# A fused attention and expert kernel whose opening issues its loads, copies and subtractions in a new order

## The chip, the cores and the metric

The kernel runs on one core of a Trainium2 chip. The metric is the device time of one execution in microseconds (us); the time before is the median of three runs. The engines are named as the profile names them: PE multiplies matrices (PEld is its weight load), DVE, ACT and POOL do elementwise work, and SP only issues transfers. POOL issues transfers too, in the order of its other instructions.

## The reference

The inputs are q, k and v of shape 8 x 8 x 576 x 64 (batch, heads, positions, width), s of 8 x 8 x 576, and the weights of eight experts. For each of the 64 pairs of batch and head it computes causal attention with a bias:

```python
s_pos = np.maximum(s, 0.0)
cum = np.cumsum(s_pos, axis=-1)
bias = -(cum[:, :, :, None] - cum[:, :, None, :])
scores = np.where(causal, -1000000000.0, scores + np.minimum(bias, 0.0))
scores = scores - np.max(scores, axis=-1, keepdims=True)
attn = np.exp(scores)
attn = attn / (np.sum(attn, axis=-1, keepdims=True) + 1e-09)
return np.matmul(attn, v).astype(np.float32)
```

The 4608 rows of the result then go to one of eight experts each (a router by cosine similarity, two matrix products, a weight per row).

## The kernel before

**Work.** The 64 pairs are called heads here, numbered 0 to 63. Four heads are a group, eight a batch. `qkb0` to `qkb2` hold q and k of a group, transposed, in rows 0 to 63; rows 64 to 127 hold the running sums of s, ones and zeros, and the row maxima that a first pass finds. q and k are used in two parts, a rounded one and the rest: `QC` and `KC` hold for each head the other combinations of the two parts. For group 0 the rest is a subtraction on chip (`klow` on POOL, `qlow` on DVE, two heads at a time: pair 0 and pair 1). For later groups ACT writes the negated rounded values (`neg`), and an adding transfer (`addl`, issued by POOL) adds the original from memory; `hcopy` writes the other half.

**A head.** `s1` to `s4` multiply q and k for the maxima, and DVE reduces them (`sr`, `max4`). After two heads `mrow1`/`mrow2` turn the maxima and `sends` has SP write them into `qkb`. `ta_`, `tb_` and `tbl` compute the shifted scores, ACT takes the exponents (`expa`, `expb1`, into P), POOL writes their low part (`pl_`, into PL, a piece of 576 columns and one of 1024), and `pv` multiplies with v, which `emm` and `vcp` have prepared. The first pass runs three to five heads ahead.

**Order.** All of it stands in a manual schedule: each engine runs its instructions in the order in which the Python code emits them. `begin()` is the opening: the setup, the first pass of heads 0 to 2 (`rows`), then a loop over heads 0 to 2 (their scores, and the first pass of heads 3 to 5) and the first pass of head 6 with `pv(0)`. From head 3 on, `step(n)` does head n's scores, the first pass of a later head, and `pv(n - 2)`. Step n of PE begins with the mask product of `ta`.

**Queues around the change.** Group 1 (heads 4 to 7) goes to `qkb1` in two transfers, k at line 949 and q after `sends()` of the first maxima. `load(2)` is group 2's, `loadc` writes the sums, `krow` a row of ones, `qones` and `kzeros` fill the rows below, `setup2` writes borders, `setup3` and `setup4` the router's constants. `vsq` sums the squares of v on ACT, `vscale` makes a scale of them, which `vcp` needs.

Of the kernel before, what the change touches and what calls it, by code (L numbers as in the profile page):

```python
# [106 lines left out]
def main(ctx, tc, qkh, qkc, vtin, s_in, emb, tau, w1h, w2h, out, shared, nb):  # L107
# [49 lines left out]
    nc.vector.memset(zero, 0.0)  # L157
    nc.vector.memset(one, 1.0)

    def kzeros(i):  # L160
        nc.vector.memset(qkbs[i][64:128, QW:].bitcast(F32), 0.0)

    def round0(i):
        nc.scalar.copy(qkbs[0][0:64, 2 * SP * i:2 * SP * i + 2 * SP], qrs[i])
# [12 lines left out]
    nc.vector.memset(tiny, 1.0e-30)  # L177
    nc.vector.memset(tri0, 0.0)
    nc.vector.memset(tri, 1.0)
    kzeros(1)  # L180
    nc.vector.tensor_scalar(st, st, 0.0, 8.0, op0=ALU.max, op1=ALU.mult)
    nc.vector.tensor_tensor_scan(cum, st, st, 0.0, op0=ALU.add, op1=ALU.bypass)
    nc.vector.tensor_copy(chl[:, 0, :], cum)
    nc.vector.tensor_sub(chl[:, 1, :], cum, chl[:, 0, :].bitcast(F32))
    for i in range(2):
        nc.sync.dma_start(qkbs[0][64 + i:65 + i, QW:].bitcast(F32), chl[0:HG, i, :].bitcast(F32))
    nc.vector.memset(ones, 1.0)

    def masks():
# [54 lines left out]
    def load(g, o=slice(0, QW + KW)):  # L244
        if g >= NGg:
            return
        qkb = qkbs[g % 3]
        if g > 0:
            nc.gpsimd.dma_start(qkb[0:64, o], qkh[g][:, o], **(dict(max_dma_last_dim=4864) if g < 3 else {}))
        G[g] = dict(QB=qkb[:, 0:QW].rearrange("p (h s) -> p h s", h=HG), KB=qkb[:, QW:].rearrange("p (h s) -> p h s", h=HG))  # L250

    def loadc(g):
        if g == 1:
            for i in range(2):
                nc.gpsimd.dma_start(qkbs[1][64 + i:65 + i, QW:].bitcast(F32), chl[HG:2 * HG, i, :].bitcast(F32))
        elif 1 < g < NGg:
            nc.sync.dma_start(qkbs[g % 3][64:66, QW:].bitcast(F32), cumd[:, HG * g:HG * (g + 1), :].rearrange("x r s -> x (r s)").bitcast(F32))
# [73 lines left out]
    def klow(i):  # L331
        h = pair(i)
        psub(KCs[0][0:64, h], krs[i].rearrange("p (h s) -> p h s", h=2), G[0]["KB"][0:64, h].bitcast(F32))

    def qlow(i):
        h = pair(i)
        nc.vector.tensor_sub(QCs[0][64:128, h], qrs[i].rearrange("p (h s) -> p h s", h=2)[:, :, 64:SP], G[0]["QB"][0:64, h, 64:SP].bitcast(F32))

    def prep(n, k):
        g, c = n // HG, n % HG  # L340
# [90 lines left out]
    def mrow1(n):  # L431
        if 0 <= n < NH and n % 2:
            rq.append(partial(mrow2, n // 2))
# [509 lines left out]
    def begin():  # L943
        make_identity(nc, ident)
        masks()
        load(0)
        loadc(1)
        nc.gpsimd.dma_start(krs[1], qkh[0][:, QW + 2 * S:])
        load(1, slice(QW, QW + KW))
        krow(0)  # L950
        krow(1)
        ra, rb, rc, rd, re = rsetup()
        rb()
        hset(0)
        for i in range(2):
            round0(i)
            hcopy(0, False, i)
            hcopy(0, True, i)
            if i == 0:
                ra()  # L960
        qlow(0)
        klow(0)
        rows(0)
        rc()
        rd()
        qones(1)
        rows(1)
        rc()
        sends()
        load(1, slice(0, QW))  # L970
        re()
        klow(1)
        for p in range(2):
            loadt(0, pair(p))
        nc.sync.dma_start(cumd.rearrange("x r s -> r x s").bitcast(F32), chl.bitcast(F32))
        rows(2)
        hset(1)
        setup2()
        neg(1, True, 0)
        neg(1, True, 1)  # L980
        for n in range(3):
            m = n + 3
            ta_(n, m)
            sr(m, 3)
            expa(n)
            if n == 0:
                vsq(0, (0, 1))
            if n == 1:
                sends()
                neg(1, False, 1)  # L990
            if n == 2:
                vscale(0)
                fslot()
                while tasks:
                    slot()
                vcp(0, False)
                vcp(1, False)
            s2(m)
            tb_(n)
            sr(m, 2)  # L1000
            sr(m, 1)
            if n == 2:
                vcp(0, True)
                vcp(1, True)
            s3(m)
            if n == 1:
                r7s[0]()
            tbl(n)
            s4(m)
            expb1(n)  # L1010
            if n == 0:
                neg(1, False, 0)
            if n == 1:
                vsq(0, (2, 3))
            if n == 2:
                hcopy(1, True, 0)
            mrow1(m)
            if n == 1:
                qlow(1)
            if n < 2:  # L1020
                pl_(n, 0, 576, "p")
                if n == 0:
                    addl(1, True, pair(0))
                pl_(n, 576, 1600, "p")
            if n == 2:
                qones(2)
            if n == 0:
                addl(1, True, pair(1))
                load(2)
            if n == 1:  # L1030
                addl(1, False)
                emm(0)
                emm(1, om)
        m = 6
        kzeros(2)
        krow(2)
        s1(m)
        sr(m, 3)
        sends()
        s2(m)  # L1040
        pv(0, [0, 1, 2])
        sr(m, 2)
        sr(m, 1)
        s3(m)
        emm(2)
        pv(0, [3, 4])
        s4(m)
        hcopy(1, True, 1)
        vcp(2, False)
        hcopy(1, False, 0)  # L1050
        vcp(2, True)
        hcopy(1, False, 1)
        loadc(2)
        loadt(1, pair(0))
        pl_(2, 0, 576, "p")

    def step(n):
        m = n + LA - (n < 6)
        live = n < NH
        b0, b1, c8 = n // H, n // H + 1, n % H  # L1060
        prev = n - 1 < NH
        g, c = n // HG, n % HG
        if live and c == 0:
            hset(g + 1)
            load(g + 2)
            loadc(g + 2)
        if n == 4:
            setup4()
            setup3()
        fslot()  # L1070
        norm1(n - 3)
        if live:
            ta_(n, m)
        if prev:
            pl_(n - 1, 576, PS(n), "p")
        sr(m, 3)
        norm2(n - 3)
        sa(m)
        if live:
            expa(n)  # L1080
            prep(n, True)
        norm3(n - 3)
        if live:
            tb_(n)
        sr(m, 2)
        s3(m)
        if live:
            tbl(n)
        mslot()
        if prev and PS(n) < 1600:  # L1090
            pl_(n - 1, PS(n), 1600, "v")
        if n < NH - 1:
            wlow()
        k = n - NH + 8
        if k > 7:
            wsq((12, 14, 14)[k - 8])
        if live:
            emm(n)
        sb(n, m)
        sbr(m)  # L1100
        if n < NH:
            tail(n)
        if n == 5:
            s1(10)
            sr(10, 3)
            s2(10)
        pv(n - 2, [0, 1, 2])
        if rq:
            rq.popleft()()
        if n == 5:  # L1110
            sr(10, 2)
            sr(10, 1)
            s3(10)
        pv(n - 2, [3, 4])
        if n == 5:
            s4(10)
        if n >= NH:
            for f in (norm1, norm2, norm3):
                f(n - 2)
            if n == NH:  # L1120
                wlow(4)
            for _ in range(9 if n == NH + 2 else 2):
                slot()
            tail(n)
        if live:
            expb1(n)
            vcp(n, False)
        aslot()
        if live:
            prep(n, False)  # L1130
            vcp(n, True)
        if n == NH - 1:
            xcv(0, 0)
            for f in (norm1, norm2, norm3):
                f(n - 2)
            for t in range(1, 3):
                xtr(0, t, pxs())
                xcv(0, t)
        if k > 0:
            wsq((0, 2, 3, 6, 8, 8, 9, 10, 12, 14, 16)[k])  # L1140
            wcv((0, 0, 0, 0, 0, 1, 2, 2, 1, 2, 0)[k], True)
        brk[0] = False
        if n < NH:
            slots(4)
        if n in (3, 4, 5):
            vsq(1, ((0,), (1,), (2, 3))[n - 3])
        if H <= n < NH and 2 <= c8 < 6 and b1 < nb:
            vsq(b1, (c8 - 2,))
        if live and c8 == 6 and b1 < nb:
            vscale(b1)  # L1150
        if n == 3:
            loadt(1, pair(1))
        if H <= n < NH and c8 < 4:
            loadt(b1, c8)
        if n == NH - 8:
            wissue(3)
        for _ in range(SCN[c8] if n < NH - 22 else n - NH + 3 if NH - 3 < n < NH else 1 + (c8 > 5) + 4 * (n > NH - 6)):
            scatter()
        later()
        if live and c == 0:  # L1160
            addl(g + 1, True)
        if live and c == 1:
            addl(g + 1, False)
        mrow1(m)
        if live:
            pl_(n, 0, 576, "p")
# [288 lines left out]
```

## Time and profile before

| | us |
|---|---|
| median of three runs | 789.05 |
| lowest and highest | 788.06, 793.63 |
| the profiled execution | 785.73 |
| its span, first to last instruction | 784.0 |

Engines busy in the span: PE 762.7 us (97%), DVE 526.6, ACT 568.0, POOL 384.3. The page's slices show PE below 90% only in the first 60 us and in the last slices. [...] In a timeline each row gives start, duration, the instruction, and in brackets how long the engine idled before it and what ended that.

### The profile page before, as it was taken

To read this page: it belongs to the slowest core of one execution; us is meant where nothing else is said; L and a number is where in the kernel's file an instruction comes from. 1 tells how busy PE (TensorE), PEld (TensorE's weight loads), DVE (VectorE), ACT (ScalarE), POOL (GpSimd) and SP (SyncE) were. 2 spreads that over 40 slices of the span, in tenths; PEclk is the share of its full clock that TensorE was granted. 3 is DMA by queue.
4 is the path that set the end of the run, shared out by engine and by line. 5 is a ranking of instruction groups with operands and counts; after the bars stand their busy time and mean duration, and the time that the engine had idled before them with its cause. 6 is when DMAs were issued, how large, how long until landed. Compare 5 with 4: busy or idle time off the path is not lost. (4 is left out here: it accounts for less than half of the span.)

```text
span 784.0 us, 19399 instructions
## 1 busy us (share of the span) xinstructions
PE 762.7 (97%) x7276; PEld 572.0 (73%) x7276; DVE 526.6 (67%) x1774; ACT 568.0 (72%) x1011; POOL 384.3 (49%) x372
## 2 busy tenths in 40 slices
PE   8679999999999999999999999999999999999997
PEld 4679999999999999996576557466465574664753
DVE  8568888888888878868675657655665466556621
ACT  9568999999999999987665866837648468376410
POOL 9847788898989798885422121220221212302001
PEclk9789999999999999999999999999999999999999
DMA  5965879798889898764724665653855557645001
GB/s 120 205 152 98 177 167 209 174 211 174 206 174 216 174 210 181 195 211 154 233 85 129 177 187 161 153 192 105 196 187 102 173 161 148 199 98 142 12 15 55
DMA packets 76096, 123.79 MB, mean 158 GB/s; under 512 B 38806, under 2 KB 39210, under 8 KB 75140
## 3 DMA queue, kind: packets, MB, share of 16 engines
q0 software_dynamic: 19728, 69.68, 37.9%
q1 hardware_dynamic: 56272, 52.84, 25.0%
q8 instruction: 58, 0.95, 0.5%
q14 instruction: 38, 0.31, 0.1%
HBM read 93.99 MB, written 21.49 MB: 147 GB/s over the span
## 5 line engine op out<-in xcount | busy, mean ns | idle before, releaser
L242 POOL TENSOR_TENSOR PL<-P 128x576 f16<-128x576 f32 (+2 forms) x128 | 206.2, 1714 | 24.8 <-ACT P L486 16.2
L852 PEld LDWEIGHTS <-wt 128*128 128x128 f16 x1536 | 149.7, 98 | 59.5 <-DVE wt L840 0.5
L852 PE MATMUL h<-xH,wt 128*128 128x320 f16 (+2 forms) x1024 | 186.7, 299 | 0.0
L882 POOL DMA_INDIRECT out<-Kx,xj x39 | 40.1, 1029 | 167.4 <-DVE Kx L881 112.4
L720 POOL DMA_INDIRECT Qx<-xs,idx x40 | 42.0, 1049 | 142.0 <-ACT hp L861 84.9
L514 PE MATMUL om<-vh,P 128*128 128x73 f16 x960 | 108.1, 199 | 0.9 <-DVE xt L539 0.6
L352 PE MATMUL s<-qkb 96*128 96x288 f32 (+4 forms) x272 | 98.3, 375 | 10.9 <-issue 5.5
L515 PE MATMUL om<-vl,P 128*128 128x72 f16 x960 | 107.3, 197 | 0.0
L516 PE MATMUL om<-vh,PL 128*128 128x73 f16 x960 | 107.1, 198 | 0.0
L852 PE MATMUL h<-xL,wt 128*128 128x320 f16 (+1 forms) x480 | 106.1, 297 | 0.0
L515 PEld LDWEIGHTS <-P 128*128 128x128 bf16 x960 | 95.3, 99 | 1.5 <-issue 0.9
L514 PEld LDWEIGHTS <-P 128*128 128x128 bf16 x960 | 94.3, 99 | 0.7 <-DVE xt L539 0.4
L876 PE MATMUL pxs<-wt,hp 128*128 128x512 f16 x351 | 94.9, 379 | 0.0
L516 PEld LDWEIGHTS <-PL 128*128 128x128 f16 x960 | 94.4, 98 | 0.0
L876 PE MATMUL pxs<-wt,hq 128*128 128x512 f16 x351 | 88.8, 379 | 0.1
L360 DVE CUSTOM_DVE_ANT_0 junk<-s,mS 128x448 bf16<-128x448 f32 (+3 forms) x144 | 74.0, 520 | 9.2 <-PE s L352 6.8
L489 ACT ACTIVATE P<-tb 128x1024 f32<-128x1024 f32 x64 | 65.1, 1017 | 6.0 <-PE tb L457 4.2
L881 DVE TENSOR_SCALAR Kx<-pxs,xj,idx 128x512 f32<-128x512 f32 x39 | 31.5, 808 | 53.2 <-PE pxs L876 37.9
L352 PEld LDWEIGHTS s<-qkb 96*128 96x128 f32 x272 | 51.9, 194 | 18.0 <-DVE M L360 9.0
L861 ACT ACTIVATE hv<-h 128x640 f16<-128x640 f32 (+2 forms) x18 | 11.6, 643 | 73.3 <-PE h L852 67.4
L876 PEld LDWEIGHTS <-hp 128*128 128x128 f16 x351 | 34.3, 98 | 41.4 <-issue 0.3
L876 PEld LDWEIGHTS <-hq 128*128 128x128 f16 x351 | 34.3, 98 | 41.2
(252 smaller groups left out, 1859.2 us busy)
## 6 DMA issues: line engine op xcount, KB each, us to landing
qkb<-qkh POOLq DMA_DIRECT2D x14, 1216.0 KB, 9.1
ring<-w2h SPq DMA_DIRECT2D x44, 256.0 KB
ring<-w1h SPq DMA_DIRECT2D x36, 256.0 KB
QC<-qkh POOLq DMA_DIRECT2D x15, 576.0 KB, 8.0
KC<-qkh POOLq DMA_DIRECT2D x14, 576.0 KB, 8.3
vT<-vtin SPq DMA_DIRECT2D x24, 320.0 KB
rw<-w1h SPq DMA_DIRECT2D x15, 256.0 KB
rw<-w2h SPq DMA_DIRECT2D x12, 256.0 KB
```

What stands on the lines that cost most here:

```text
L242: nc.gpsimd.tensor_tensor(out, a, b_, op=ALU.subtract)
L352: nc.tensor.matmul(out, G[g]["QB"][0:96, h, 128 * i:128 * i + 128], G[g]["KB"][0:96, h, lo:hi], start=True, stop=True)
L360: nc.vector.tensor_tensor_reduce(out=jk, in0=src, in1=ms, scale=1.0, scalar=NEG, op0=ALU.add, op1=ALU.max, accum_out=MP[n // 2][:, n % 2, ...
L489: nc.scalar.activation(HD[n]["P32"][:, 576:1600], HD[n]["tb"], AF.Exp, scale=0.125)
L514: nc.tensor.matmul(out, lh, vh[:, kb], start=(kb == 0), stop=False)
L515: nc.tensor.matmul(out[:, u:u + 72], lh, vl[:, kb], start=False, stop=False)
L516: nc.tensor.matmul(out, ll, vh[:, kb], start=False, stop=(kb == j))
L720: ins = nc.gpsimd.indirect_dma_start(out=x.bitcast(I32), out_offset=None, in_=src, in_offset=bass.IndirectOffsetOnAxis(ap=X[("i", e, t)][1 ...
L852: nc.tensor.matmul(h[:, u, 0:b - a], w[:, 128 * c:128 * c + 128], x[:, c, lo + a:lo + b], start=(c == 0 and k == 0), stop=(c == 3 and k == 2))
L876: nc.tensor.matmul(y, h[:, 128 * t:128 * t + 128], w, start=(m == 0 and k == 0), stop=(m == 7 and k == 2))
L881: nc.vector.tensor_scalar(ys, y, xf[3], IX["RS"][:, 2 * e + 1:2 * e + 2], op0=ALU.mult, op1=ALU.mult)
L882: nc.gpsimd.indirect_dma_start(out=out, out_offset=bass.IndirectOffsetOnAxis(ap=xf[0].bitcast(U32), axis=0), in_=ys, in_offset=None, bound ...
```

## The change

The opening issues its work in another order; nothing is computed differently.

- On DVE the zeros of `qkb1` (`kzeros(1)`) come after the running sums instead of before them.
- Group 1 is one transfer of q and k at the place where k's was, ahead of the small `loadc` transfers.
- `qlow(1)` moves from DVE to POOL, to right behind `klow(1)`, and `kzeros(2)` from DVE to POOL, behind `qones(2)`.
- The adding transfers of group 1 go by pair: k and q of pair 0 around the first low part of head 0, k and q of pair 1 at the end of head 2's turn; ACT's negations move with them. `setup2` moves behind the first of these.
- `load(2)` stays between the low parts of heads 0 and 1; what POOL does ahead of it changes.
- `vsq`, `vcp`, `emm(2)` move later or earlier by some places; `load(3)` moves from the start of step 4 into it, `setup3`/`setup4` from step 4 to step 10, batch 1's `vsq` from steps 3 to 5 to steps 4 to 6, its `vscale` from the end of step 6 into step 7.

```diff
+    def kzeros(i, e=nc.vector):
+        e.memset(qkbs[i][64:128, QW:].bitcast(F32), 0.0)
...
-    kzeros(1)
     nc.vector.tensor_scalar(st, st, 0.0, 8.0, op0=ALU.max, op1=ALU.mult)
...
+    kzeros(1)
     nc.vector.memset(ones, 1.0)
...
         load(0)
+        nc.gpsimd.dma_start(krs[1], qkh[0][:, QW + 2 * S:])
+        load(1)
         loadc(1)
-        nc.gpsimd.dma_start(krs[1], qkh[0][:, QW + 2 * S:])
-        load(1, slice(QW, QW + KW))
...
-        load(1, slice(0, QW))
         re()
         klow(1)
+        qlow(1, nc.gpsimd)
...
-        setup2()
         neg(1, True, 0)
-        neg(1, True, 1)
+        neg(1, False, 0)
...
-            if n == 0:
-                vsq(0, (0, 1))
...
-            if n == 1:
-                vsq(0, (2, 3))
+            if n < 2:
+                vsq(0, (2 * n, 2 * n + 1))
             if n == 2:
+                neg(1, True, 1)
+                neg(1, False, 1)
                 hcopy(1, True, 0)
             mrow1(m)
+            if n == 2:
+                vcp(0, True)
+                vcp(1, True)
+            if n == 0:
+                addl(1, True, pair(0))
+                pl_(n, 0, 576, "p")
+                addl(1, False, pair(0))
+                setup2()
+                pl_(n, 576, 1600, "p")
             if n == 1:
-                qlow(1)
-            if n < 2:
+                load(2)
                 pl_(n, 0, 576, "p")
...
             if n == 2:
                 qones(2)
+                kzeros(2, nc.gpsimd)
+                krow(2)
                 addl(1, True, pair(1))
+                addl(1, False, pair(1))
         m = 6
-        kzeros(2)
-        krow(2)
...
         s2(m)
+        emm(2)
+        vcp(2, False)
         pv(0, [0, 1, 2])
...
+            if n > 4:
+                load(g + 2)
+                loadc(g + 2)
-        if n == 4:
+        if n == 10:
             setup4()
             setup3()
```

On POOL, near the start (names: `vh` is the buffer that first takes k of heads 2 and 3, `qkb_93` is `qkb1`, `P_87` holds the sums):

```order
 L193 COPY trim<-trim 128x64
 L194 IOTA ebase 128x8
+L947 DMA vh_107<-qkh 64x1152
+L249 DMA qkb_93<-qkh 64x4x1216
 L255 DMA qkb_93<-P_87 1x4x576 x2
-L948 DMA vh_107<-qkh 64x1152
-L249 DMA qkb_93<-qkh 64x2x1152
 L171 DMA qkb_92<-qkc 1x16x144
 L171 DMA qkb_93<-qkc 1x16x144
```

The whole of group 1 now stands ahead of the small rows of sums and ones; the transfer of q, `64x4x640`, is gone from its place behind `qones(1)`.

On POOL, from `klow(1)` to group 2's load, before (`KC_90`: group 0, `KC_91`: group 1, `qkb_94`: `qkb2`; the two blocks of `setup2` between the first two rows are left out by beginning behind them):

```order
L242 TENSOR_TENSOR PL_109<-P_85 128x576
L329 DMA KC_91<-qkh 64x2x576
L242 TENSOR_TENSOR PL_109<-P_85 128x1024
L329 DMA KC_91<-qkh 64x2x576
L249 DMA qkb_94<-qkh 64x4x1216
L242 TENSOR_TENSOR PL_110<-P_86 128x576
```

and now, up to the start of `setup2`:

```order
L242 TENSOR_TENSOR KC_90<-vh_107,qkb_92 64x1152
L337 TENSOR_TENSOR QC_88<-vT_96,qkb_92 64x1152
L329 DMA KC_91<-qkh 64x2x576
L242 TENSOR_TENSOR PL_109<-P_85 128x576
L329 DMA QC_89<-qkh 64x2x576
L203 MEMSET onesb 128x128
```

The subtraction for q stands ahead of all low parts. `setup2` (15 small instructions from L203 on) and the piece of 1024 columns follow, then the load of `qkb_94`.

On POOL, behind that load, now:

```order
L249 DMA qkb_94<-qkh 64x4x1216
L242 TENSOR_TENSOR PL_110<-P_86 128x576
L242 TENSOR_TENSOR PL_110<-P_86 128x1024
L168 MEMSET qkb_94 64x2560
L161 MEMSET qkb_94 64x2304
L171 DMA qkb_94<-qkc 1x16x144
L329 DMA KC_91<-qkh 64x2x576
L329 DMA QC_89<-qkh 64x2x576
L242 TENSOR_TENSOR PL_111<-P_87 128x576
```

The memset at L161 came from DVE, and two adding transfers stand ahead of head 2's low part (`PL_111`) where none stood before.

## Rows read from the trace of the kernel before

**Rows 1.** Windows: length, busy PE, PEld, DVE, ACT, POOL (count), PE clock, DMA share, GB/s.
```profile
26.50:35.50 9.00, 9.00 (x38) 8.32 (x39) 5.40 (x15) 5.37 (x8) 6.59 (x6) 0.50 0.88 145
...
44.50:49.70 5.20, 5.20 (x55) 5.02 (x55) 1.33 (x6) 1.44 (x2) 3.08 (x3) 0.51 0.54 158
...
100.00:120.00 20.00, 20.00 (x299) 19.59 (x299) 16.29 (x72) 18.38 (x25) 18.91 (x15) 1.00 0.77 172
```

**Rows 2.** Timeline of PE, 19 to 57 us: start, duration, instruction, idle before.
```profile
19.14 0.54 PE L450 MATMUL tb<-qkb 128*128 128x448 f32 x2
...
20.72 0.28 PE L457 MATMUL ta<-trim,identb 128*128 128x256 bf16 x1
26.50 0.71 PE L352 MATMUL s<-qkb 96*128 96x448 f32 x1 [5.50 <-issue]
...
28.61 0.90 PE L450 MATMUL tb<-qkb 128*128 128x448 f32 x2
...
40.35 0.47 PE L352 MATMUL s<-qkb 96*128 96x448 f32 x1 [0.94 <-DVE M L397]
...
44.47 0.80 PE L352 MATMUL s<-qkb 96*128 96x320 f32 x2 [2.90 <-DVE M L360]
...
49.88 0.29 PE L457 MATMUL ta<-trim,identb 128*128 128x256 bf16 x1
...
53.66 0.21 PE L514 MATMUL om<-vh,P 128*128 128x73 f16 x1
...
55.19 0.27 PE L457 MATMUL ta<-trim,identb 128*128 128x256 bf16 x1
...
56.20 0.52 PE L450 MATMUL tb<-qkb 128*128 128x448 f32 x2
```

**Rows 3.** DMA view, 0 to 60 us: issues, KB each, median us to landing.
```profile
qkb<-qkh POOLq DMA_DIRECT2D x1, 640.0 KB, 9.3
```

**Rows 4.** Timeline of DVE, 0 to 62 us.
```profile
33.38 3.08 DVE L337 TENSOR_TENSOR QC<-vT,qkb 64x1152 fp32r<-64x1152 f32 x1
...
41.77 1.98 DVE L161 MEMSET qkb<- 64x2304 f32 x1 [0.54 <-issue]
```

**Rows 5.** Timeline of POOL, 0 to 62 us.
```profile
9.24 0.66 POOL L249 DMA_DIRECT2D qkb<-qkh  x1
...
17.05 0.72 POOL L249 DMA_DIRECT2D qkb<-qkh  x1
...
19.78 2.61 POOL L242 TENSOR_TENSOR KC<-vh,qkb 64x1152 fp32r<-64x1152 f32 x1
22.34 0.19 POOL L203 MEMSET onesb<- 128x128 bf16 x1
...
24.09 1.17 POOL L242 TENSOR_TENSOR PL<-P 128x576 f16<-128x576 f32 x1
25.18 1.06 POOL L329 DMA_DIRECT2D KC<-qkh  x1
25.95 2.24 POOL L242 TENSOR_TENSOR PL<-P 128x1024 f16<-128x1024 f32 x1
...
36.24 2.23 POOL L168 MEMSET qkb<- 64x2560 f32 x1
```

**Rows 6.** The page, DMA issues: KB each, median us to landing.
```profile
qkb<-qkh POOLq DMA_DIRECT2D x14, 1216.0 KB, 9.1
```

**Rows 7.** Everything on the tile qkb, 0 to 90 us.
```profile
DMA to landing us min/median/max: 1.7/5.6/12.7
```

**Rows 8.** Groups by line and shape, 50 to 250 us: busy us, mean ns.
```profile
L242 POOL TENSOR_TENSOR PL<-P 128x1024 f16<-128x1024 f32 x39 | 81.1, 2079 | 4.6 <-ACT P L489 4.5
L242 POOL TENSOR_TENSOR PL<-P 128x576 f16<-128x576 f32 x40 | 56.6, 1415 | 10.6 <-ACT P L486 10.6
...
L489 ACT ACTIVATE P<-tb 128x1024 f32<-128x1024 f32 x40 | 40.7, 1017 | 1.3 <-PE tb L457 0.6
...
L321 ACT ACTIVATE KC<-qkb 64x1152 fp32r<-64x1152 f32 x20 | 23.0, 1152 | 0.0
```

More of the change, by code (lines that the diff above doesn't have):

```diff
@@ L158, in main @@
     nc.vector.memset(one, 1.0)
-    def kzeros(i):
-        nc.vector.memset(qkbs[i][64:128, QW:].bitcast(F32), 0.0)
+    def kzeros(i, e=nc.vector):
+        e.memset(qkbs[i][64:128, QW:].bitcast(F32), 0.0)
     def round0(i):
@@ L333, in klow, with qlow @@
         psub(KCs[0][0:64, h], krs[i].rearrange("p (h s) -> p h s", h=2), G[0]["KB"][0:64, h].bitcast(F32))
-    def qlow(i):
+    def qlow(i, e=nc.vector):
         h = pair(i)
-        nc.vector.tensor_sub(QCs[0][64:128, h], qrs[i].rearrange("p (h s) -> p h s", h=2)[:, :, 64:SP], G[0]["QB"][0:64, h, 64:SP].bitcast(F32))
+        e.tensor_sub(QCs[0][64:128, h], qrs[i].rearrange("p (h s) -> p h s", h=2)[:, :, 64:SP], G[0]["QB"][0:64, h, 64:SP].bitcast(F32))
     def prep(n, k):
@@ L985, in begin @@
             expa(n)
-            if n == 0:
-                vsq(0, (0, 1))
             if n == 1:
                 sends()
-                neg(1, False, 1)
             if n == 2:
@@ L1001, in begin @@
             sr(m, 1)
-            if n == 2:
-                vcp(0, True)
-                vcp(1, True)
             s3(m)
@@ L1010, in begin @@
             expb1(n)
-            if n == 0:
-                neg(1, False, 0)
-            if n == 1:
-                vsq(0, (2, 3))
+            if n < 2:
+                vsq(0, (2 * n, 2 * n + 1))
             if n == 2:
+                neg(1, True, 1)
+                neg(1, False, 1)
                 hcopy(1, True, 0)
             mrow1(m)
+            if n == 2:
[7 more added lines that the diff above has]
+                pl_(n, 576, 1600, "p")
             if n == 1:
-                qlow(1)
-            if n < 2:
+                load(2)
                 pl_(n, 0, 576, "p")
-                if n == 0:
-                    addl(1, True, pair(0))
                 pl_(n, 576, 1600, "p")
+                emm(0)
+                emm(1, om)
             if n == 2:
                 qones(2)
-            if n == 0:
+                kzeros(2, nc.gpsimd)
+                krow(2)
                 addl(1, True, pair(1))
[L1029 to L1033, printed above, removed]
+                addl(1, False, pair(1))
         m = 6
-        kzeros(2)
-        krow(2)
         s1(m)
@@ L1043, in begin @@
         sr(m, 1)
+        vcp(2, True)
         s3(m)
-        emm(2)
         pv(0, [3, 4])
         s4(m)
+        hcopy(1, False, 0)
         hcopy(1, True, 1)
-        vcp(2, False)
-        hcopy(1, False, 0)
-        vcp(2, True)
         hcopy(1, False, 1)
@@ L1064, in step @@
             hset(g + 1)
-            load(g + 2)
-            loadc(g + 2)
-        if n == 4:
+            if n > 4:
+                load(g + 2)
+                loadc(g + 2)
+        if n == 10:
             setup4()
@@ L1106, in step @@
             s2(10)
+        if n == 7:
+            vscale(1)
         pv(n - 2, [0, 1, 2])
+        if n == 7:
+            fslot()
         if rq:
             rq.popleft()()
+        if n == 4:
+            load(3)
+            loadc(3)
         if n == 5:
@@ L1144, in step @@
             slots(4)
-        if n in (3, 4, 5):
-            vsq(1, ((0,), (1,), (2, 3))[n - 3])
+        if n in (4, 5, 6):
+            vsq(1, ((0,), (1, 2), (3,))[n - 4])
         if H <= n < NH and 2 <= c8 < 6 and b1 < nb:
             vsq(b1, (c8 - 2,))
-        if live and c8 == 6 and b1 < nb:
+        if live and c8 == 6 and 1 < b1 < nb:
             vscale(b1)
```

## The prediction

> **What bounds the kernel now.** I read the windows first, to see which engine has no slack. In the steady part PE is busy 20.00 of 20.00 us and POOL 18.91 [rows 1], and ACT's exponent of 1024 columns, one per step, comes 40 times in 200 us [rows 8]: a step takes 5.0 us, set by PE, and whatever delays PE in the opening is added to the end. So the question is how much earlier PE reaches its steady steps.
>
> Then the timeline of PE in the first 57 us [rows 2]. The reader is to see two holes and what follows them. PE writes the mask of head 1 at 20.72, is done at 21.00, and starts the next product, the first that reads group 1, at 26.50. That hole of 5.50 is put down to "issue", but q of group 1 was issued at 17.05 [rows 5] and took 9.3 us [rows 3], which lands at 26.35: it is the load. The second hole ends at 44.47, after 2.90 us of waiting for DVE, which from 41.77 filled zeros for 1.98 [rows 4]. After each hole the granted clock is at the lower level, 0.50 from 26.5 to 35.5 and 0.51 from 44.5 to 49.7 [rows 1]. Step 3 begins at 49.88 and step 4 at 55.19 [rows 2].
>
> **The change, and what it is worth.** The sum goes by when PE begins step 3, and then by who is late in steps 3 and 4.
>
> *Group 1's load.* All of it now goes where k's part went, at 9.24 or sooner [rows 5]. A load of this size takes 9.1 us at the median of 14 [rows 6] and 12.7 at most [rows 7]: it lands at 18.3, at the latest at 21.9. I take 18.3; the 12.7 is a load that was issued behind adding transfers such as that of 25.18 [rows 5]. PE needs it at 21.0: the hole of 5.50 goes. What is late next is a free bank of scores, which DVE's reductions of head 3 hold: an estimated 0.7, so 21.7.
>
> *The clock.* Without the hole I expect the full clock to stay. The same pair of products takes 0.90 at the low level and 0.54 at the full one [rows 2], a factor 1.67, where the clock alone says 2.0 [rows 1]; I take 1.8. The stretch of 9.0 us then takes 5.0, and that of 5.2 takes 2.9.
>
> *DVE's part.* `qlow(1)` leaves DVE (3.08 [rows 4]), and so do the zeros of `qkb2` (1.98). I count neither by itself: they show in the holes. In the pass of head 6 PE still waits for DVE. From the end of head 5's scores at 39.41 (40.35 less its wait of 0.94) to 44.47 there are 5.1 us; of these the 2.90 shrink to an estimated 1.2, since DVE now does two low parts of v there instead of earlier, so 3.3 are left. The stretch between, 35.5 to 39.4, I leave at 3.9.
>
> *Step 3* then begins at 21.7 + 5.0 + 3.9 + 3.3 + 2.9 = 36.8, against 49.88: 13.1 sooner.
>
> *POOL, which takes the moved work.* It is the chain that can eat this. Before, `klow(1)` ended at 22.34 [rows 5]; without q's transfer (0.72 at 17.05) it ends at 21.6. `qlow(1)` has the shape of `klow(1)`, 2.61: 24.2. An adding transfer holds POOL from 25.18 to 25.95, 0.77: 25.0. The first low part of head 0, 1.42 on the mean [rows 8]: 26.4; the second adding transfer: 27.2; `setup2`, from 22.34 to 24.09 before, 1.75: 28.9; the second low part, 2.08 [rows 8]: 31.0. There group 2's load is issued (28.42 before, if 25.95 and the transfers behind it are added up, so 2.6 later), and it lands 9.1 later, at 40.1. On goes POOL with 0.66 for the issue, 3.5 for head 1, `qones(2)` 2.23 [rows 5], and the zeros, which no row shows on POOL: a gain is excluded, as the work is new there; above, the wider fill of ones took 2.23, and DVE's row is 1.98. I take 2.0, nearest to 2.23 by width (2304 to 2560 columns). With 0.5 for a small and 1.5 for two adding transfers, and 3.5 for head 2: 44.9.
>
> *Steps 3 and 4.* Step 3 at its old length of 5.3 puts step 4 at 42.1. Three things must be there. Group 2 at 42.1 for PE, and earlier for ACT, whose negation stands ahead of head 3's second exponent: 40.1 + 1.15 + 1.02 [rows 8] = 42.3, needed by the product that comes 1.0 after the step's start (56.20 less 55.19 [rows 2]), at 43.1. Head 2's low part at 44.9, needed 3.8 after the start (53.66 less 49.88), at 45.9. Both are in time by about 1. The third is ACT itself: `vsq` of batch 0 now follows the exponents, and pair 1's two negations and four copies stand ahead of head 3's exponents, 6 x 1.15 = 6.9. ACT has caught up when it ends 0.4 later than step 3 would like. I put this at 0.4 as an estimate, between nothing and the 2.1 of a whole negation with an exponent.
>
> *The rest.* Moving batch 1's `vsq` by one step, `vscale` behind it, and the constants to step 10 costs nothing: the constants cover no wait of PE, and ACT is busy 18.38 of 20.00 us in the steady part [rows 1], 4.6 in a step of 5.0; if that cover were gone, one `vsq` of about 0.9 would show. On SP the sums of group 2 now wait until POOL has filled the zeros, at 39.9, and behind them are the loads of batch 1's values, needed at the end of step 4.
>
> Sum: 13.1 - 0.4 = **12.7 us** sooner, and all of it lasts, as the steps behind are bound by PE. On the profiled execution's 785.73 that gives 773.0. That execution stands 3.3 below the median of the runs, 789.05, from which I take the same 12.7: **776.4**. The ends: with the longest load for group 2 (12.7 instead of 9.1) ACT is ready 3.6 later and the gain is 9.1; with nothing late it is 13.7.
>
> [...]
>
> **The rivals.**
>
> *The clock falls although the hole is gone.* PE in the opening is not dense: between 39.4 and 44.5 it worked in bits, and after that it ran at 0.51 [rows 1]. If it falls at about 24 and stays low for 9 us, as it did before, the 4.0 that I took from that stretch are given back in part: 12.7 - 4.0 = 8.7, and 6.5 if the second stretch stays low too. For it: heads 1 and 2 have waits for DVE in them. Against it: none that I find is longer than 1.6 us. Time 780 to 783.
> [...]
>
> *The first load is not sooner where it counts.* It now shares the stretch behind 9.24 with k of heads 2 and 3, and the rows of ones for head 0 queue behind it. If it takes the 12.7 of rows 7, it lands at 21.9, and the rows of ones only then; they are needed by head 0's scores at about 18.3. PE then waits 3.6, with the clock down behind it: 12.7 - 3.6 - 4.0 = 5.1 sooner, 784. For it: 14 loads have a median of 9.1 but one had 12.7. Against it: little else is in flight there.
>
> *POOL becomes the bound, and the kernel slower.* POOL takes over 4.6 us of work and is then late, while it has 18.91 of 20.00 us to do in the steady part [rows 1], 4.73 per step. If a denser DVE beside it stretched its instructions by 15%, a step would need 5.44, each of some 50 steps would lose 0.44, and the time would be 776.4 + 22 = 798. It decides from 5.0 us of POOL per step on, 6% above now. For it: its instructions do vary, the piece of 576 columns took 1.17 at 24.09 [rows 5] and takes 1.42 on the mean [rows 8]. Against it: in those 40 steps POOL idled for 10.6 and 4.5 us waiting for ACT's exponents [rows 8], so it catches up.
>
> **How the numbers follow.** The forecast, a gain of 9.1 to 13.7, gets 0.78; the clock 0.10; the late first load 0.07; POOL 0.05. The range is 771 to 784: the low end is 785.73 less 13.7 and a us for the spread, since the runs may come out nearer to the profiled execution than to the median; the high end is the second rival. A measurement of this kernel can tell about 1% from no change, 7.9 us. Faster by more than that: 0.78 and half of the clock's 0.10, 0.83. Within it: the other half and the late load, 0.12. Slower: 0.05.
>
> **What would show it.** Right: no hole at the first product of group 1, which starts near 21.7; a granted clock of 1.00 all through; step 3 near 37 and step 4 near 42; group 2's load issued near 31. ACT's negation for group 2 ends near 41. Wrong: PE idle for over 2 us anywhere behind 18; the clock at 0.50 for more than 5 us; steps of more than 5.0 us after step 13 or PE waiting for POOL in `pv`.

## The result, and the profile after

The changed kernel takes **779.78 us** (median of 6, 777.59 to 782.62) where the kernel before, run beside it, takes 789.63 (6 runs, 788.06 to 794.57): ratio 0.9862, 95% interval 0.9823 to 0.9900, so 9.85 us sooner. Forecast were 776.4, a range of 771 to 784, and 12.7 us. Experiments came in three later series, on three chips, each with the kernel before beside it: its median was 784.24 in series 2 (`b_load1`, `b_kz2`, `a_again`, `a_wlow`), 785.50 in series 3 (`b_again`, `a_ld3`, `a_ld3l`, `a_qdve`) and 787.95 in series 4 (`b_both`, `b_ld2`, `a_kz1`, `a_best`). Times are compared within a series only; the first result is series 1.

The profiled execution is the one of 777.59 (span 775.9). The timeline of PE, to set against [rows 2]: start, duration, instruction, idle before it.

```profile
19.14 0.27 PE L457 MATMUL ta<-trim,identb 128*128 128x256 bf16 x1
...
22.03 0.29 PE L457 MATMUL ta<-trim,identb 128*128 128x256 bf16 x1
22.08 0.44 PE L352 MATMUL s<-qkb 96*128 96x448 f32 x1
...
33.72 0.50 PE L352 MATMUL s<-qkb 96*128 96x320 f32 x2 [1.27 <-DVE M L360]
...
36.80 0.28 PE L457 MATMUL ta<-trim,identb 128*128 128x256 bf16 x1
...
43.02 0.27 PE L457 MATMUL ta<-trim,identb 128*128 128x256 bf16 x1 [1.02 <-ACT P L489]
```

The masks of heads 0, 1, 3 and 4 stand at 19.14, 22.03, 36.80 and 43.02. The hole of 5.50 is gone, and the wait of 2.90 for DVE is now 1.27. Step 3 is 13.1 sooner than the 49.88 of before, step 4 12.2. But head 0 begins 1.3 later than in the kernel before, whose row is

```profile
17.80 0.27 PE L457 MATMUL ta<-trim,identb 128*128 128x256 bf16 x1
```

DVE's zeros of the second buffer now stand behind the running sums, in the way of the first maxima; `a_kz1` tests that. The changed kernel's windows, columns as in [rows 1]:

```profile
19.00:27.00 8.00, 7.70 (x57) 6.63 (x56) 6.40 (x30) 5.61 (x10) 7.86 (x5) 1.00 0.64 206
27.00:37.00 10.00, 7.88 (x88) 6.70 (x86) 6.86 (x30) 9.15 (x15) 9.70 (x22) 1.00 0.82 135
37.00:50.00 13.00, 11.98 (x155) 11.39 (x155) 9.45 (x41) 11.75 (x15) 12.63 (x11) 1.00 0.85 191
100.00:120.00 20.00, 20.00 (x305) 19.78 (x302) 16.00 (x73) 17.31 (x21) 19.17 (x18) 1.00 0.82 187
```

The granted clock (the column ahead of the last two) is 1.00, the full level, in all four windows; the stretches ahead of 19 and from 50 to 70 have 1.00 too. POOL's timeline, against [rows 5]:

```profile
22.85 2.65 POOL L337 TENSOR_TENSOR QC<-vT,qkb 64x1152 fp32r<-64x1152 f32 x1
...
30.45 1.91 POOL L242 TENSOR_TENSOR PL<-P 128x1024 f16<-128x1024 f32 x1
32.29 0.67 POOL L249 DMA_DIRECT2D qkb<-qkh  x1
...
38.21 2.02 POOL L161 MEMSET qkb<- 64x2304 f32 x1
```

q's second subtraction takes 2.65 on POOL (2.61 taken), the zeros 2.02 (2.0 taken), and group 2's load is issued at 32.29 (31.0 forecast, the 1.3 of the late opening). ACT's timeline shows when the loads were there:

```profile
17.57 1.16 ACT L321 ACTIVATE KC<-qkb 64x1152 fp32r<-64x1152 f32 x1 [0.84 <-DMA qkb<-qkh]
...
40.89 1.17 ACT L321 ACTIVATE KC<-qkb 64x1152 fp32r<-64x1152 f32 x1 [1.14 <-DMA qkb<-qkh]
41.96 1.00 ACT L489 ACTIVATE P<-tb 128x1024 f32<-128x1024 f32 x1
```

Group 1's load lands at 17.5 (18.3 forecast), group 2's at 40.9 (40.1). The exponent at 41.96, late by ACT's wait of 1.14, is what PE waits 1.02 for at step 4.

Step 13, in the trace of before and in this one:

```profile
101.86 0.28 PE L457 MATMUL ta<-trim,identb 128*128 128x256 bf16 x1
```
```profile
90.32 0.28 PE L457 MATMUL ta<-trim,identb 128*128 128x256 bf16 x1
```

It is 11.5 sooner. Of the 12.2 of step 4, 0.2 went by step 5 and a net 0.5 between the starts of steps 6 and 8, where batch 1's `vscale` (`sc`) now stands in step 7 and PE waits for it:

```profile
64.72 0.19 PE L514 MATMUL om<-vh,P 128*128 128x73 f16 x1 [0.30 <-DVE sc L907]
```

The two spans, 784.0 and 775.9, differ by 8.1 only: of the 11.5, 0.8 goes at steps 47 to 49, 0.3 more up to the last step, and 2.3 where the experts begin. The experiments below show that this late loss comes with the series, not with the change.

### The profile page after: what moved, and what is told of

It is laid out like the page before. It is cut to its first block, busy times and chain, and to the rows that moved or that the text cites. A ratio compares the mean times of both kernels' runs of the same rounds, so it can differ in the third digit from the quotient of the medians.

```text
span 775.9 us, 19400 instructions
## 1 busy us (share of the span) xinstructions
PE 758.8 (98%) x7276; PEld 566.0 (73%) x7276; DVE 524.4 (68%) x1772; ACT 567.9 (73%) x1011; POOL 388.0 (50%) x374
## 5 line engine op out<-in xcount | busy, mean ns | idle before, releaser
L352 PE MATMUL s<-qkb 96*128 96x288 f32 (+4 forms) x272 | 96.4, 367 | 2.9 <-DVE M L360 2.2
L454 PE MATMUL tb<-QC,KC 128*128 128x448 f32 (+3 forms) x256 | 63.6, 307 | 0.0
```

The costliest lines, as they stand in the source:

```text
L352: nc.tensor.matmul(out, G[g]["QB"][0:96, h, 128 * i:128 * i + 128], G[g]["KB"][0:96, h, lo:hi], start=True, stop=True)
L454: nc.tensor.matmul(out, HD[n]["KC"][:, ks:ks + 128], HD[n]["QC"][:, qlo:qhi], start=False, stop=stop)
```

## The experiments

**Does the execution repeat?** `a_again` is the changed kernel unaltered, in series 2.

> The changed kernel once more, unaltered. Theory (the loss behind step 13 is a fixed meeting of DVE's low part of the weights with POOL's low part at 337 us): that DVE instruction takes 3.75 us again, the shift against before is 11.5 at step 13 and 8 at the first expert product, ratio 0.986 to 0.990. Rival (the loss is chance between executions): the DVE instruction takes near 0.75 in this execution, and the shift at the end is 10 or more.

Six runs: 773.86, 773.86, 774.14, and 778.70, 778.75, 778.99; median 776.42, ratio 0.9884 (0.9848 to 0.9920). The mean granted clock goes with it: 0.997 to 0.999 in the first three, 0.992 to 0.993 in the others. The profiled one is of the second kind, and its row in question takes 0.74, not 3.75: the theory of a fixed meeting fell. There is no late loss at all (7.0 sooner at step 13 and 7.0 at the end). What was lost lies at head 6: step 6 began 10.7 us sooner than in the trace of before, step 7 only 7.6. Its timelines of POOL, SP and PE, and from the DMA view the load's KB and us to landing:

```profile
48.89 0.59 POOL L249 DMA_DIRECT2D qkb<-qkh  x1
...
49.43 0.76 SPq L443 DMA_DIRECT2D qkb<-mr  x1
...
58.39 0.57 PE L450 MATMUL ta<-qkb 128*128 128x256 f32 x2 [1.89 <-DMA qkb<-mr]
```
```profile
qkb<-qkh POOLq DMA_DIRECT2D x1, 1216.0 KB, 9.1
```

SP sends 5 KB of maxima (`mr`) 0.54 us after POOL has issued group 3's load. The load lands at 48.89 + 9.1 = 58.0, and PE, which needs the maxima, goes on at 58.39. In the execution of 777.59 the order is the other way round (timelines of SP, POOL and PE):

```profile
48.08 0.76 SPq L443 DMA_DIRECT2D qkb<-mr  x1
...
49.05 0.59 POOL L249 DMA_DIRECT2D qkb<-qkh  x1
...
54.99 0.43 PE L450 MATMUL ta<-qkb 128*128 128x256 f32 x2
```

PE doesn't wait. `a_wlow`, whose order differs only at heads 62 and 63, gives the other kind in the same series (774.54): there too the maxima went first, at 48.36 against 49.23, and PE did not wait. It is 1.2 sooner than `a_again`'s at step 4 and 4.3 at step 13, so about 3 of these are lost at head 6, the rest in the opening.

That gave a new theory: **a small transfer sent just behind a large load is done only when the load is**, and which goes first is decided by tenths of a us. The trace shows the order of the two, 0.54 apart, and that PE goes on 0.4 after the load has landed; no row shows what makes the maxima wait.

One place in the trace of before does not fit the order of the rows (POOL, SP, PE): the maxima of heads 2 and 3 were sent 0.31 behind the start of group 2's load, which landed 12.7 later, near 41.1, and yet PE took them at 35.46 without a wait.

```profile
28.42 1.36 POOL L249 DMA_DIRECT2D qkb<-qkh  x1
```
```profile
28.73 0.77 SPq L443 DMA_DIRECT2D qkb<-mr  x1
```
```profile
35.46 0.63 PE L450 MATMUL ta<-qkb 128*128 128x256 f32 x2
```

So the starts of the two rows don't decide alone; what does is open. The maxima that were sent ahead of a load, by 0.97 in the execution of 777.59 and by 0.87 in `a_wlow`, did not wait for it.

**The same in the kernel before.** `b_again` is the kernel before unaltered, one run in series 3.

> The kernel before once more, unaltered, for a second profiled execution. Theory (its executions differ by whether a row of maxima from SP lands behind a load of 1216 KB that POOL issues within a us of it, and by the half clock behind each wait): the opening differs by a whole wait of PE or by a stretch of 0.50 clock, step 3 between 43 and 52, and the mean clock goes with it, 0.993 where step 3 is early and 0.983 where it is late; behind step 13 the two executions run alike to 0.5 us. Rival (the executions differ all along, by a different pace of the steps): the shift against the first execution grows or shrinks by over 2 us between step 13 and the end.

It took 784.63. Timelines of POOL, SP and PE:

```profile
17.07 0.72 POOL L249 DMA_DIRECT2D qkb<-qkh  x1
...
17.13 0.78 SPq L443 DMA_DIRECT2D qkb<-mr  x1
...
23.14 0.36 PE L450 MATMUL ta<-qkb 128*128 128x256 f32 x1 [3.95 <-DMA qkb<-mr]
```

In the execution ahead of the prediction the maxima of heads 0 and 1 went at 16.24, ahead of that load of q at 17.05 [rows 5], and nothing waited. Here they came 0.06 behind and PE waited 3.95 in head 0. Step 3 came 1.2 sooner all the same: the first product of group 1 (26.90) has no hole ahead of it, so one wait stood in for the 5.50. Another wait grew: q's second subtraction took 3.67 us on DVE behind two low parts of POOL, and PE waited 2.80 for it where before it waited 0.52.

```profile
35.73 0.50 PE L454 MATMUL ta<-QC,KC 128*128 128x320 f32 x2 [2.80 <-DVE QC L337]
```

From step 3 to the end the two run alike to 0.1 us. Executions of one kernel differ in the opening, then, and the rival fell.

**Moving the load against the maxima.** `a_ld3` undoes one part of the change: group 3's load returns to the beginning of step 4, ahead of the maxima. `a_ld3l` moves it the other way, and with it the adding transfer of group 2's keys.

```diff
# a_ld3
-            if n > 4:
-                load(g + 2)
-                loadc(g + 2)
+            load(g + 2)
+            loadc(g + 2)
...
-        if n == 4:
-            load(3)
-            loadc(3)
# a_ld3l: step 4's load(3), loadc(3) and addl(2, True) now here
         if live:
             pl_(n, 0, 576, "p")
+        if n == 4:
+            load(3)
+            loadc(3)
+            addl(2, True)
```

> The changed kernel with one of its parts undone: group 3's load goes back to the beginning of step 4. There POOL reaches it some 2 us sooner, near 47.0 instead of 49.0, and the maxima of heads 6 and 7, which SP sends at 48.1 to 49.4, now follow it in every execution. Theory (a small transfer behind the load lands when the load does): they land near 56 always, PE waits 0.5 to 1.5 us at the first product of head 6, and the times no longer fall in two clusters 4.9 us apart (773.9 and 778.8); they lie between, near 776, within 2 us of each other. Rival A (small transfers don't queue behind the load): no wait there, two clusters as before from another cause. Rival B (the clusters come from the clock at 35 to 40 us): two clusters stay, at 774 and 779.

> The changed kernel with group 3's load and the adding transfer of group 2's keys (both in step 4) moved behind POOL's next low part of 576 columns: issued near 51 instead of 49, so that the maxima of heads 6 and 7, sent at 48.1 to 49.4, always go first. Theory (a small transfer ahead of the load lands at once): no wait of PE for the maxima in any execution, one cluster near 774, clock 0.997 or more; group 3 lands near 60.5, which the first product of head 12 needs at 60.3, so at most 1 us is given back there. Rival (clusters come from the clock at 35 to 40 us): half of the runs stay at 779.

`a_ld3` (timelines of POOL, SP and PE):

```profile
47.11 0.59 POOL L249 DMA_DIRECT2D qkb<-qkh  x1
...
48.02 0.76 SPq L443 DMA_DIRECT2D qkb<-mr  x1
...
57.38 0.60 PE L450 MATMUL ta<-qkb 128*128 128x256 f32 x2 [2.27 <-DMA qkb<-mr]
```

The load took 9.9, so it landed at 57.0, and PE went on at 57.38. The wait was more than expected (0.5 to 1.5), and the six runs form one group at 776.72 to 779.25, median 777.80; ratio 0.9885 (0.9848 to 0.9923). `a_ld3l`:

```profile
49.60 0.75 SPq L443 DMA_DIRECT2D qkb<-mr  x1
...
50.13 0.59 POOL L249 DMA_DIRECT2D qkb<-qkh  x1
...
56.52 0.43 PE L450 MATMUL ta<-qkb 128*128 128x256 f32 x2
```

No wait, five of six runs at 774.10 to 775.75, one at 778.00; median 774.47, ratio 0.9851 (0.9811 to 0.9890). By the medians of this series the load ahead of the maxima is 3.3 us slower than behind them. The theory held but for the one run at 778.00, Rival A of `a_ld3` fell, and the rival of `a_ld3l` too, though in its profiled execution the clock did fall (0.66 at 35 to 40 us); it stands 1.1 to 1.6 above the other four of its group. In `a_ld3` the adding transfer came behind the maxima, and in `b_again` none stood beside them, so the wait does not need that transfer.

**The two holes of before, apart and together.** In the kernel before, `b_load1` loads all of group 1 where only k went, ahead of the small sums as in the change, `b_kz2` fills the third buffer's zeros on POOL, `b_both` does both.

```diff
# b_load1
+        nc.gpsimd.dma_start(krs[1], qkh[0][:, QW + 2 * S:])
+        load(1)
         loadc(1)
-        nc.gpsimd.dma_start(krs[1], qkh[0][:, QW + 2 * S:])
-        load(1, slice(QW, QW + KW))
...
-        load(1, slice(0, QW))
# b_kz2, with kzeros(i, e=nc.vector) as in the change
-        kzeros(2)
+        kzeros(2, nc.gpsimd)
```

> The kernel before with one part of the change: all of group 1 is loaded where before only k's part was. Theory (a hole costs its wait and the slow clock behind it): no hole at the first product of group 1, which starts near 21.7; granted clock 1.00 from there to the zeros' hole, so the stretch of 9.0 us at 0.50 takes about 5; DVE's zeros still hold up head 6, so a wait of 2 to 3 us near 35 and a half clock behind it remain. Step 3 at 42 or so against 49.88, and 7 to 8 us sooner from there on: about 0.991 of the time before. Rival A (a hole costs its wait alone, the clock falls anyway): 5 us or less sooner, step 3 at 45, clock 0.50 somewhere between 22 and 31. Rival B (the load takes 12.7 beside the others): a wait of over 2 us for it stays.

> The kernel before with one other part of the change: the zeros of the third buffer are filled by POOL, not DVE. Theory: the wait of 2.90 ahead of head 6 shrinks below 1.2 and the clock does not fall behind it, so the stretch of 5.2 us at 0.51 takes about 2.9: step 3 at 45 against 49.88, 4 to 5 us sooner, about 0.994 of the time before; the first hole of 5.5 and its half clock stay as they were. Rival A (the wait alone counts): 1.7 to 2.9 sooner, clock near 0.5 behind 44.5 still. Rival B (POOL is then late with group 2's load or the low parts): PE waits for POOL or ACT in steps 3 to 5 and the gain is under 2.

> The kernel before with both parts together: all of group 1 loaded early, and the zeros of the third buffer on POOL. Theory (the change's gain is these two holes and little else, and they add): the fastest runs of the two alone stand 4.0 and 2.9 below the fastest of the kernel before, so 6.9 together, 0.991 to 0.992, fastest runs near 775.5; no hole at the first product of group 1 and no wait of over 1.3 for DVE at head 6. Rival A (without the rest of the new order, POOL's later low parts and group 2's load become the next wait): PE waits 2 us or more for POOL or a load between 33 and 55, 4 us together and no more than the load alone. Rival B (the rest of the order counts as well as these): the whole change's 8 to 9 us are reached here too, 773.9.

| | median | fastest | beside it: before, median and fastest | ratio |
|---|---|---|---|---|
| `b_load1` | 778.95 | 778.29 | 784.24, 782.31 | 0.9926 (0.9893 to 0.9958) |
| `b_kz2` | 782.00 | 779.45 | 784.24, 782.31 | 0.9961 (0.9934 to 0.9987) |
| `b_both` | 781.57 | 778.83 | 787.95, 785.99 | 0.9921 (0.9892 to 0.9949) |

By their fastest runs: 4.0, 2.9, and together 7.2; by their medians 5.3, 2.2 and 6.4. That the two add up fits the first and not the second, and `b_both`'s fastest stands 2.6 below its other three, so it is not shown. `b_load1` has no hole at the first product of group 1 (21.09); it kept a wait of 2.90 at head 6 (ahead of 37.66; the row names a load of `qkb` there, not DVE) and a clock of 0.66 at 35 to 45, and is 6.5 sooner from step 3 on. Its first stretch did not stay full either (0.66 at 25 to 30). `b_kz2`'s profiled execution, the slowest of its ten runs, has 0.27 in place of the 2.90 and gained nothing: its maxima of heads 2 and 3 fell behind group 2's load (timelines of POOL, SP and PE).

```profile
28.42 1.36 POOL L249 DMA_DIRECT2D qkb<-qkh  x1
...
28.86 0.77 SPq L443 DMA_DIRECT2D qkb<-mr  x1
...
40.39 0.58 PE L450 MATMUL ta<-qkb 128*128 128x256 f32 x1 [4.59 <-DMA qkb<-mr]
```

`b_both`'s profiled execution, its fastest, has both holes gone and is 10.7 us sooner at step 13, near the whole change's 11.5, with none of the rest:

```profile
24.49 0.62 PE L450 MATMUL tb<-qkb 128*128 128x448 f32 x2 [1.15 <-ACT P L489]
...
35.35 0.50 PE L352 MATMUL s<-qkb 96*128 96x320 f32 x2 [0.27 <-DVE M L360]
...
91.14 0.28 PE L457 MATMUL ta<-trim,identb 128*128 128x256 bf16 x1
```

The rest is not idle, though. With the hole gone PE waits 1.15 for ACT's exponent of head 0, which stands behind the first `vsq`, and the clock is 0.67 at 25 to 30; the changed kernel, with that `vsq` behind the exponent, has neither and goes from the mask of head 1 to step 3 in 14.8 us where `b_both` takes 17.2. Against `b_both` it gives back 0.8 by a later start (the zeros) and 0.8 at steps 4 to 8. Rival A fell. Rival B can't be told from the theory by ratios: 0.9921 and the 0.9884 of `a_again` have intervals that overlap.

**The scatter of before, by one edit.** `b_ld2` issues group 2's load behind the next low part, near 31.

```diff
-                load(2)
...
                 if n == 0:
                     addl(1, True, pair(0))
+                else:
+                    load(2)
                 pl_(n, 576, 1600, "p")
```

> The kernel before with one edit: group 2's load is issued behind POOL's next low part, near 31 instead of 28.4, so that the maxima of heads 2 and 3, which SP sends at 28.6 to 28.9, go first. Theory (its runs scatter from 782 to 791 because a small transfer now and then lands behind a load issued within a us of it): no wait of PE for these maxima; the runs of 786 and more become rarer, median 782 to 783, lowest unchanged at 782. The other such pair, at 17.1, stays and may still cost 4 us in some runs. Rival (the scatter has another cause): the runs spread as those of the kernel before, median within 0.7 of it.

Median 786.96, 785.00 to 789.30; before beside it reached 794.92. Ratio 0.9981 (0.9954 to 1.0007). The upper end narrowed, but ten runs don't prove it: inconclusive. In its profiled execution the other pair, at 17.05 and 17.11, cost PE 3.72, as foreseen.

**The late loss.** The order of `b_ld2` behind the opening is that of before, and yet from step 13 to the end it loses 3.6. So do `b_both` (3.8) and `a_kz1` (5.0), of the same series (`a_kz1` though DVE's row of the weights takes 0.74 in it); `a_best`, whose tail is altered, loses 1.7. The eight profiled executions of series 2 and 3 lose none. The profiled execution of before has none, and at 785.73 lies below all six runs of series 1. The lowest run of before is 788.06 and 785.99 in series 1 and 4, 782.31 and 782.65 in 2 and 3. So the late loss seen with the result is not the change's: it comes with a series. Its cause is open; the later series ran on different chips, and no run separates the chip from the time of the series.

**q's second subtraction.** `a_qdve` gives it back to DVE.

```diff
-        qlow(1, nc.gpsimd)
...
             if n == 1:
+                qlow(1)
                 load(2)
```

> The changed kernel with one of its parts undone: q's second subtraction goes back from POOL to DVE, into the step of head 1. Theory (DVE with two inputs is held as long as POOL runs beside it, and PE waits for DVE in the opening): that DVE instruction takes 2.5 to 3.1 us beside POOL's work instead of 1.35, PE waits 1 to 2 us more for DVE between 28 and 36, and POOL issues group 2's load 2.6 sooner, near 29.6; since that load was late by about 1 us at step 4 at most, the net is 0.5 to 2 us slower than the changed kernel: 0.990 against before. Rival A (DVE has room there, POOL is the one that is late): 0.5 to 1.5 us faster than the changed kernel. Rival B: the wait brings the half clock, 3 us or more slower.

Ratio 0.9871 (0.9822 to 0.9921), median 776.14, within the interval of `a_again`. The DVE instruction took 2.12, less than expected, and PE waited 0.6 for it. POOL was sooner and group 3's load too (46.42), so the maxima, at 48.98, fell behind that and an adding transfer: 0.86. In these runs this part of the change is worth less than can be measured, either way; the wait of 2.80 in `b_again` shows what it can prevent.

**The zeros of the second buffer.** `a_kz1` puts them ahead of the sums again.

```diff
     nc.vector.memset(tri, 1.0)
+    kzeros(1)
...
-    kzeros(1)
     nc.vector.memset(ones, 1.0)
```

> The changed kernel with one of its parts undone: DVE fills the zeros of the second buffer ahead of the running sums again, not behind them. Theory (behind the sums these 1.98 us stand in the way of q's first subtraction and of the first maxima, which PE waits for): PE's transpose of the first maxima comes at 15.6 instead of 16.9, the granted clock at 15 to 20 is 1.00 instead of 0.67 to 0.83, and the times come 1.3 to 2 us lower than the changed kernel's: fastest runs near 772.3, ratio 0.985 to 0.987. Rival (hidden, since PE catches up by step 3): within 0.5 us of the changed kernel, fastest runs 773.9.

Of `a_kz1` PE's timeline and window, then of the changed kernel's profiled run of series 1 PE's row and of `a_wlow` (same order of zeros) the window:

```profile
15.37 0.27 PE L438 MATMUL pm<-ident,M 128*10 128x128 f32 x1 [1.52 <-DVE es L578]
```
```profile
15.00:20.00 5.00, 4.38 (x26) 3.34 (x27) 4.09 (x20) 4.47 (x5) 4.79 (x4) 1.00 0.69 149
```
```profile
16.92 0.27 PE L438 MATMUL pm<-ident,M 128*10 128x128 f32 x1 [1.81 <-DVE es L578]
```
```profile
15.00:20.00 5.00, 3.20 (x12) 1.94 (x11) 3.85 (x18) 4.21 (x4) 4.56 (x7) 0.74 0.49 65
```

The opening is 1.55 sooner and the clock 1.00. All eight profiled executions with the zeros ahead have 1.00 there; of the six with the zeros behind the sums, five have 0.67 to 0.83 and the one of the result has 1.00. Step 13 is 12.5 sooner than in before's trace (11.5 in the result's). The time, 777.65, ratio 0.9872 (0.9840 to 0.9905), is within the changed kernel's interval; the fastest of its four runs lies 9.15 below the fastest of before, for `a_again` in series 2 that figure is 8.45. The later start is shown, its worth in the time is not.

**The weights' low part.** `a_wlow` lets DVE make it a step later.

```diff
-        if n < NH - 1:
+        if n < NH - 2:
             wlow()
+        if n == NH - 1:
+            wlow(1)
```

> The changed kernel with one edit far from the opening: the low part of the weights that DVE makes in the step of head 62 is made in that of head 63, so that it does not meet POOL's low part of 1024 columns. Theory (a DVE instruction with two inputs from SBUF waits as long as POOL's runs beside it): no 3.75 us row of that line; the end is 2 to 3 us sooner than the unaltered changed kernel's, ratio 0.983 to 0.986 against before, shift at the first expert product 10 or more. Rival (the 3.75 is hidden or the order of the weights matters more): end within 0.7 us of the unaltered changed kernel's in the trace, and the shift at the first expert product stays near 8.

Median 774.41, ratio 0.9875 (0.9843 to 0.9907). The step of 11.3 at step 13 lasts to the end (11.2), but `a_again` lost nothing there either, and the instruction still met POOL (1.92 us). By its fastest run, 774.21 against 773.86, the edit is worth nothing in this series: the theory isn't borne out, and the better median comes from one run in six in the upper cluster instead of three.

**The three edits together.** `a_best` is `a_ld3l` with those of `a_kz1` and `a_wlow`.

> The changed kernel with three edits: group 3's load and the adding transfer beside it behind POOL's next low part, the zeros of the second buffer ahead of the sums again, and DVE's low part of the weights one step later. Theory: the first removes the slow half of the runs (one cluster), the second gives 1.3 to 2 us, the third keeps DVE clear of POOL near 337 us: median 772.5, ratio 0.983 to 0.984, no row of 3.75 us in that line of DVE. Rival: the second is hidden, median 774.3 as with the first alone.

Five runs at 774.71 to 775.30, against 787.95: ratio **0.9835** (0.9811 to 0.9859), 12.9 us sooner than before. There is one cluster within 0.6 us, as in the theory (its median of 772.5 was reckoned from a kernel before at 785.5), and the profiled maxima went first: sent at 47.50, load at 49.25. The ratio is the one expected. The rival, that the zeros are hidden, isn't ruled out by it, since the interval of `a_ld3l` (0.9851) overlaps; DVE's row of the weights took 1.10, still beside POOL.

## Why the prediction was right, and where it failed

**Right.** The bound was PE's opening, and the hole for group 1 and the zeros' hole were most of what the change took away: `b_both` alone has 10.7 of the 11.5 us at step 13, best execution against best. The landing of the load, q's subtraction and the zeros on POOL were within 0.8. POOL, the rival that would have made it slower, never held PE in the profiled execution.

**Right by luck.** Step 3 was forecast at 36.8 and came at 36.80 by errors that cancel: the opening began 1.3 later than the sum knew, the wait of 0.7 for a bank of scores did not come, and the terms 5.0, 3.9, 3.3 and 2.9 came out near 5.6, 3.6, 2.5 and 3.1. And it is this execution's figure: in the five others of series 2 and 3 with the zeros behind the sums step 3 stands at 38.0 to 39.7. The gain of 13.7 behind the low end of the range is not worked out: with nothing late the sum gives 13.1.

**The step that failed** is the end of the sum, "and all of it lasts". Of 12.7 us, 9.85 were measured in series 1, and 9.1 by the ratio of series 2. The profiled execution had 11.5 left at step 13: ACT cost 0.9 at step 4 where the sum has 0.4, and moving batch 1's `vsq` and `vscale`, which "costs nothing" there, brought PE the wait of 0.30 in step 7 in all eight profiled executions of that order: steps 6 and 7 take 10.95 us in the five of them without a wait for maxima there, 10.50 before. Three more things stand in its place.

1. *A move without a price.* Group 3's load went from the beginning of step 4 to its middle, and the sum has no term for it, though SP sends the maxima of heads 6 and 7 beside it, 48.1 to 49.4. `a_again`'s profiled execution, with the load first, stands in an upper cluster, 4.9 above the other and at the lower clock, with two more of its six runs. With the load moved ahead (`a_ld3`) the wait came and there was one cluster; with it moved behind (`a_ld3l`) there was none and five of six runs were low. On SP the prediction had looked at the sums of group 2 alone.
2. *One execution taken for the kernel.* The waits of 5.50 and 2.90 are those of an execution of 785.73. `b_again` had a wait of 3.95 in another place, and the runs of before in series 2 go from 782.31 to 791.03. The fastest of `a_again` stands 8.45 below the fastest of before in its series.
3. *The order on DVE.* Zeros behind the sums cost 1.3 at the start of head 0 in the profiled execution, and 2.0 to 3.1 in the five others, where the clock fell at 15 to 20 us. The prediction shows no term for it.

**The clock.** That it stays full was right in the profiled execution. `a_again` had 0.78 at 15 to 20, where PE had just waited 1.81 for DVE, and 0.67 at 35 to 40, behind a stretch in which PE was busy 3.2 of 5 us. The execution of 777.59 had the same wait and 3.25 of 5 us, and 1.00 in both places, so what decides is open. Its price can be read: from the mask of head 1 to step 3 it is 14.8 us where the clock stayed at 1.00 behind 25 us (four executions, the result's among them) and 16.4 where it fell near 35 (`a_again`, `a_ld3l`, `a_best`). The first rival named this, with 780 to 783; here it comes in some executions, in short pieces.

**ACT** was later at step 4 than the 0.4 of the sum: PE waited 1.02, since group 2's load was issued 1.3 late. In the five others, where step 3 came later, that wait is gone.

## What to carry to other kernels

Before moving a large load, list the small transfers that any queue sends near its new place, and put the load behind them: a race of tenths of a us cost waits of 1.9 to 4.6 us here, in some executions and not in others. In `a_ld3l`'s trace 0.5 us behind was enough. Where runs of one kernel fall in clusters, take a second profile of it before costing anything from the first. In an opening bound by one engine, look at every instruction put ahead of that engine's first input: 1.98 us of zeros made it 1.55 later here.

## What the runs showed of the hardware

Two instructions of DVE, the row of the weights (L840) and q's subtraction (L337), took longer in some of the places where POOL's ran beside them. The row of the weights in the changed kernel, beside POOL in series 1 (DVE and POOL timelines), and then in `a_again`, where POOL had a DMA to issue:

```profile
337.42 3.75 DVE L840 SCALAR_TENSOR_TENSOR wt<-rw,idx,wt 128x512 f16<-128x512 f32 x1
...
337.61 3.00 POOL L242 TENSOR_TENSOR PL<-P 128x576 f16<-128x576 f32 x2
```
```profile
340.81 0.74 DVE L840 SCALAR_TENSOR_TENSOR wt<-rw,idx,wt 128x512 f16<-128x512 f32 x1
```

POOL ends at 340.61, DVE at 341.17, 0.56 later; in `a_wlow` 340.55 and 341.10, in `b_ld2` 348.05 and 348.61. q's subtraction took 1.35 at 8.45 in the trace of before; the 3.08 at 33.38 [rows 4] end 1.21 after the low part of POOL beside it, at 36.46 and 35.25, so an estimated 1.7 of them (3.08 less 1.35) were a wait for POOL. That the condition is two inputs from SBUF, as the expectations of `a_wlow` and `a_qdve` have it, was the author's assumption; no run shows it. In `b_ld2` POOL's was the one that took longer: DVE began 0.23 ahead and took its 1.35, and POOL's piece took 2.87, where the piece of that size ahead of it took 1.88.

```profile
31.51 1.35 DVE L337 TENSOR_TENSOR QC<-vT,qkb 64x1152 fp32r<-64x1152 f32 x1
```
```profile
31.74 2.87 POOL L242 TENSOR_TENSOR PL<-P 128x1024 f16<-128x1024 f32 x1
```

In the first fence above DVE's record begins 0.19 ahead of POOL's too, and yet it ends after both of POOL's instructions. What decides is open.
